# Every chunk of the wide layer is folded with six TensorE passes, and the scheduler's durations and offsets are fitted anew

## The chip, the cores and the metric

The program runs on one core of one Trainium2 chip. The metric is the device time of one execution in microseconds (us). Three runs of the kernel before took 1496.97, 1497.91 and 1501.18 us, a median of 1497.91.

## What is computed

The reference takes the real part of a two-dimensional FFT of eight batches of 3072 tokens by 256 columns, and feeds it to a wide layer and a soft mixture of eight experts:

```python
X = np.fft.fft(np.fft.fft(x, axis=1), axis=2).real        # 8 x 3072 x 256
h = X @ w_in;  g = h - np.tanh(h);  x = g @ w_out         # 256 -> 2048 -> 256
logits = x @ phi                                          # 32 slots
d = softmax of logits over the tokens;  slot_input = d.T @ x
slot_out[e] = relu(slot_input[e] @ w1[e]) @ w2[e]         # 8 experts of 4 slots
out = (softmax of logits over the slots) @ slot_out
```

## The kernel before, in words

The work has a head (weights are unpacked and combined), a main loop over 96 tiles (8 batches of 12), and a tail (experts, second softmax, output).

**A tile.** For every batch GpSimd (POOL) runs 24-point butterflies over the tokens in SBUF (`dft24`, recorded at L328, with scalings on ScalarE at L332). `z_dft` (L412 to L421) then makes one tile of 128 frequencies on TensorE. The input is real, so a tile stands for 128 tokens and their 128 mirrored tokens. Its two halves are the cosine part and the sine part of the columns; `z_high` and `z_low` split each into a high and a low float32r half.

**The wide layer.** It is done in four chunks of 512 columns per tile; a chunk's number is g, 384 in all, and its place in the tile is c = g % 4. With P the product of the cosine part and Q that of the sine part, the hidden values of a token and of its mirror are P + Q and P - Q. A product costs three passes of 512 columns on TensorE (high by high, high by low, low by high; `passes`, L463). There are two ways:

- *Folded*, three chunks in four: `wide` makes P (tile `pp`, doubled weights) and Q (`qq`) by three passes each. VectorE adds the term of column 128 to P (`evac`, L484) and makes the first sum (`plus`, L489); GpSimd subtracts to get the second (`minus`, L492). ScalarE takes tanh of both from SBUF (L501).
- *Whole*, the chunk with c = `FOLD` = 1: TensorE sums P + Q and P - Q itself, six passes for each, the second with sign-flipped weights `Wm`. ScalarE takes tanh in PSUM (L498). VectorE and GpSimd have nothing to do up to here.

Then, for every chunk and both signs, ScalarE writes the high float16 half of tanh (`act_t`, L509) and VectorE the low one (`low_t`, L513) into the ring `tr`. A DMA transpose on SyncE's queue (L517) turns the chunk into `tt`, and TensorE adds 16 small products to the logits (L544). After four chunks `slots` (L651) weighs the tile into the accumulator `ta`; every second tile the running softmax over tokens is carried on (L556 to L655). One of its instructions is `nm` (L589), a VectorE instruction on one column whose operands all lie in SBUF.

**What sets the order.** Every engine works through its own list in order. The lists are written when the program is built: the class `Flow` gets each operation with a duration, the rings of buffers that it takes and frees, and a place in a queue (`SCHED` holds one offset in chunks for each kind; `XLEAD`, `XSTEP`, `XEARLY`, `XFIRST` and `DSTEPS` place the loads and the butterflies of the next batch). It starts, again and again, the operation that can begin first by those durations. `HB` and `PB` are the numbers of buffers for the two sums (`h`) and for P (`pb`); `WB` is that of the PSUM banks that `pp` and `qq` may hold.

Of the kernel before, what the change touches and what calls it, by code (L numbers as in the profile page):

```python
# [46 lines left out]
SCHED = {
    "soft_t": 14.651, "logits": 6.337, "slots": 17.971, "soft_d": 16.201, "z_slots": 18.711, "z_turn": -1.458,
    "wide0": -0.165, "wide1": 0.725, "z_dft": -5.304, "ls_sum": 13.614, "soft_m": 15.558, "soft_h": 17.152,
    "soft_l": 17.462, "z_acc": 25.423, "evac": 1.54, "z_high": -2.259, "z_low": -1.816, "z_copy": -1.578,  # L50
    "z_turned": 1.314, "low_t0": 4.303, "low_t1": 5.258, "plus": 1.66, "minus": 2.729, "soft_e": 16.122,
    "ls_keep": 15.142, "act_h0": 2.255, "act_h1": 3.898, "act_t0": 3.417, "act_t1": 3.987, "acc_add": 28.127,
    "soft_x": 14.416,
# [173 lines left out]
def fft_mlp_softmoe_kernel(ctx: ExitStack, tc: tile.TileContext, x, w_in, w_out, phi, w1, w2, cq, fd, cm, ct, out):  # L227
# [439 lines left out]
    def s_wide():  # L667
        pp = pqs["S"] = bank("ppS", "pp")
        for n in range(4):
            for c in range(4):  # L670
                fs = slice(512 * c, 512 * c + 512)
                z, w = spec[0:1, 1, :], None
                if n < 2:
                    z, w = spec[:, 0, :], (Wh, Wl)[n][:, 0, fs].bitcast(F32)
                elif c == FOLD:
                    w = (Wh, Wl)[n - 2][0:1, 1, fs].bitcast(F32)
                elif n == 2:
                    w = W128[0:1, c - (c > FOLD), :]
                if w is not None:
                    nt.matmul(pp[32 * c:32 * c + 32, :], z, w, start=(n == 0), stop=(n == 2 + (c == FOLD)), tile_position=(0, 32 * c))  # L680

# [939 lines left out]
```

## Time and profile before

| | |
|---|---|
| median of three runs | 1497.91 us (1496.97 to 1501.18) |
| span of the profiled execution | 1494.0 us |
| head, until the first transposes of chunks | about 98 us |
| main loop | about 98 to 1353 us |
| tail | about 1353 to 1494 us |
| granted TensorE clock, mean | 0.983 (1.00 in the main loop) |

The span runs from the first to the last instruction of the profiled execution; the runs' times also hold what lies before and after it. A timeline row gives the start and the duration of an instruction. Durations of neighbours on one engine overlap: the next one starts before the one before has drained. What an instruction takes from its engine is the distance between starts, which is somewhat shorter than its duration.

### The profile page before, as it was taken

How to read it: one execution, taken by the hardware profiler on the slowest of the kernel's cores; microseconds unless marked ns; L12 is line 12 of the kernel's file. 1: busy time of each engine (PE TensorE's matmuls, PEld its weight loads, DVE VectorE, ACT ScalarE, POOL GpSimd, SP SyncE). 2: the span in 40 equal slices, each digit the busy share in tenths (PEclk: the TensorE clock that was granted, in tenths of full speed). 3: DMA queues.
4: the chain of work that ended last, by engine and by line, in shares of the span. 5: the costliest groups of instructions: out<-in, count | busy, mean ns of one | idle time of the engine just before them, and what ended most of it. 6: DMA issues, size and time to landing. Idle time of an engine off the chain costs nothing.

```text
span 1494.0 us, 38014 instructions
## 1 busy us (share of the span) xinstructions
PE 1410.3 (94%) x14636; PEld 1038.6 (70%) x14636; DVE 1170.2 (78%) x2041; ACT 1132.9 (76%) x2523; POOL 1012.2 (68%) x768
## 2 busy tenths in 40 slices
PE   4899999999999999999999999999999999996886
PEld 2577777777777777777777777777777776773464
DVE  7978878878878887888878788887878887783562
ACT  3467878878888778878887888878888877772476
POOL 5955799679968994899579956997599632231430
PEclk9999999999999999999999999999999999997898
DMA  7469999899999999999999999999999999899778
GB/s 229 138 155 198 195 202 196 149 193 179 195 178 197 177 187 185 187 180 188 178 184 191 186 187 176 201 169 190 171 193 181 199 188 186 156 199 294 243 296 366
DMA packets 856869, 292.90 MB, mean 196 GB/s; under 512 B 803440, under 2 KB 847344, under 8 KB 854896
## 3 DMA queue, kind: packets, MB, share of 16 engines
q1 hardware_dynamic: 856688, 290.47, 98.3%
q8 instruction: 115, 1.88, 0.5%
q14 instruction: 66, 0.54, 0.1%
HBM read 58.15 MB, written 30.67 MB: 59 GB/s over the span
## 4 chain that ended last, share of the span: by engine, by line
PE 85%; DVE 5%; DMA 5%; issue 2%; ACT 1%; SPq 0%; DVEq 0%
PE qq L463 22%; PE pp L463 22%; PE L L544 11%; PE ta L651 9%; DMA tt<-tr 3%; PE op L1546 3%; PE L L537 2%; PE tps L451 2%; PE zps L412 1%; PE zps L415 1%; PE zps L414 1%; PE zps L413 1%; PE LT L581 1%; PE zlp L635 1%; PE L L538 1%
## 5 line engine op out<-in xcount | busy, mean ns | idle before, releaser
L492 POOL TENSOR_TENSOR h<-pb,h 128x512 f32<-128x512 f32 x288 | 372.2, 1294 | 301.0 <-DVE h L489 289.2
L513 DVE SCALAR_TENSOR_TENSOR tr<-th,tr 128x512 f16<-128x512 f32 x576 | 382.3, 683 | 40.1 <-ACT tr L509 38.8
L463 PE MATMUL pp<-Wh,zh 128*128 128x512 f32 x960 | 374.3, 406 | 1.7 <-DVE tr L513 1.2
L501 ACT ACTIVATE th<-h 128x512 f32<-128x512 f32 x576 | 337.1, 607 | 38.9 <-DVE h L489 31.1
L509 ACT ACTIVATE tr<-th 128x512 f16<-128x512 f32 x576 | 335.3, 601 | 18.1 <-PE ta L651 8.4
L463 PE MATMUL qq<-Wh,zh 128*128 128x512 f32 x768 | 329.1, 428 | 3.6 <-DVE tr L513 3.5
L484 DVE SCALAR_TENSOR_TENSOR pb<-W,zts,pp 128x512 f32<-128x512 f32 x288 | 213.7, 742 | 54.2 <-PE pp L463 41.8
L489 DVE SCALAR_TENSOR_TENSOR h<-pb,qq 128x512 f32<-128x512 f32 x288 | 196.0, 681 | 64.5 <-PE qq L463 59.1
L544 PEld LDWEIGHTS <-tt 128*128 128x128 f16 x6144 | 194.0, 96 | 64.7 <-issue 49.2
L544 PE MATMUL L<-WPn,tt 128*128 128x64 f16 (+1 forms) x6144 | 225.8, 184 | 11.1 <-DMA tt<-tr 11.1
L463 PEld LDWEIGHTS pp<-Wh,zh 128*128 128x128 f32 x960 | 180.4, 188 | 46.1 <-DVE tr L513 5.3
L463 PE MATMUL pp<-Wl,zh 128*128 128x512 f32 x480 | 190.3, 396 | 0.0
L463 PEld LDWEIGHTS qq<-Wh,zh 128*128 128x128 f32 x768 | 145.0, 189 | 31.4 <-ACT zts L455 5.6
L328 POOL TENSOR_TENSOR xb<-xb 128x508 f32<-128x508 f32 (+3 forms) x103 | 146.2, 1422 | 30.0 <-DMA xb<-in_x 14.6
L463 PE MATMUL qq<-Wl,zh 128*128 128x512 f32 x384 | 151.4, 394 | 0.0
L651 PE MATMUL ta<-tr,dh 128*32 128x512 f16 x2304 | 145.3, 388 | 0.0
L442 ACT CAST zh<-zps 128x256 fp32r<-128x256 f32 x96 | 35.9, 374 | 100.3 <-PE zps L415 88.3
L651 PEld LDWEIGHTS <-dh 128*32 128x32 f16 x2304 | 54.4, 98 | 77.5 <-issue 32.8
L328 POOL TENSOR_TENSOR tA<-xb 128x1024 f32<-128x1024 f32 (+2 forms) x70 | 105.7, 1519 | 3.9 <-ACT xb L332 3.3
L463 PEld LDWEIGHTS pp<-Wl,zh 128*128 128x128 f32 x480 | 90.8, 189 | 14.8
L328 POOL TENSOR_TENSOR xb<-tA 128x508 f32<-128x508 f32 (+2 forms) x79 | 83.2, 1060 | 0.5
L463 PE MATMUL qq<-Wm,zh 128*128 128x512 f32 x288 | 83.3, 398 | 0.0
(266 smaller groups left out, 2448.3 us busy)
## 6 DMA issues: line engine op xcount, KB each, us to landing
out<-xb SPq DMA_DIRECT2D x14, 1536.0 KB, 6.2
xb<-in_x SPq DMA_DIRECT2D x32, 512.0 KB, 5.1
tr<-in_moe_w SPq DMA_DIRECT2D x16, 512.0 KB, 9.0
tt<-tr SPq DMA_TRANSPOSE x385, 4.9
xb<-in_moe_w SPq DMA_DIRECT2D x12, 512.0 KB, 4.4
raw<-in_moe_w_in SPq DMA_DIRECT2D x8, 512.0 KB, 3.6
xb<-in_x SPq DMA_DIRECT2D x16, 256.0 KB, 3.8
raw<-in_moe_w_out SPq DMA_DIRECT2D x8, 512.0 KB, 3.8
```

Of the source, the lines that this page charges most:

```text
L328: fn = lambda e: e.tensor_tensor(out=out[1](), in0=a[1](), in1=c[1](), op=op)
L442: ns.copy(out=z[1], in_=zpp[i])
L463: nt.matmul(o, z, v, start=first and n == 0, stop=last and n == 2)
L484: nv.scalar_tensor_tensor(out=pb, in0=W128[:, c - (c > FOLD), :], scalar=zs[i][3][:, 129:130], in1=pqs.pop((g, 0)), op0=ALU.mult, op1=ALU.add)
L489: nv.scalar_tensor_tensor(out=hs[g][:, 0, :], in0=pbs[g], scalar=0.5, in1=pqs.pop((g, 1)), op0=ALU.mult, op1=ALU.add)
L492: ng.tensor_tensor(out=hs[g][:, 1, :], in0=pbs.pop(g), in1=hs[g][:, 0, :], op=ALU.subtract)
L501: ns.activation(out=o, in_=hs[g][:, k, :], func=AF.Tanh)
L509: ns.activation(out=place_t(g)[:, 0, k], in_=ths[g, k], func=AF.Copy, scale=T14)
L513: nv.scalar_tensor_tensor(out=t[:, 1, k], in0=ths.pop((g, k)), scalar=T14, in1=t[:, 0, k], op0=ALU.mult, op1=ALU.subtract)
L544: nt.matmul(L[:, pm].rearrange("p b s -> p (b s)")[:, 0:n], tt[:, hl, pm, f, :], WPn[:, 4 * c + f].rearrange("p b s -> p (b s)")[:, 0:n], ...
L651: nt.matmul(tas[p][32 * c:32 * c + 32, :], dhl[p][:, dl, 2 * k + pm, :], ts[c][:, tl, pm, :], start=(k == 0 and n == 0), stop=(i == tiles( ...
L1546: nt.matmul(o.rearrange("p r d -> p (r d)"), c[:, j, :], R[:, 3 * h + k:3 * h + k + 2, :].rearrange("p r d -> p (r d)"), start=(h == 0), s ...
```

## The change

`whole`, the chunk of 12 passes, its weights `Wm` and its ways through `act_h`, `evac` and the scheduler go; `wide`, `evac`, `plus` and `minus` run for all 384 chunks. `W128` gets a fourth block. The freed SBUF holds a third buffer `pb` (`PB` 2 to 3). The durations that `Flow` reckons with, the offsets in `SCHED` and the places of loads and butterflies are other numbers, so all engines' lists are in another order. In the tail, two small tiles lie in other buffers.

```diff
-DSTEPS = 34.034
-XLEAD = -11.824
-XSTEP = 0.527
-XEARLY = 6.193
-XFIRST = 3.579
+DSTEPS = 17.994
+XLEAD = -7.457
+XSTEP = -11.057
+XEARLY = 36.171
+XFIRST = 11.84
 SCHED = {
...
-PB = 2
+PB = 3
...
-    def passes(o, zh, zl, w, first, last):
+    def passes(o, zh, zl, w):
         for n, (z, v) in enumerate(((zh, w[0]), (zh, w[1]), (zl, w[0]))):
-            nt.matmul(o, z, v, start=first and n == 0, stop=last and n == 2)
-
-    def whole(g):
-        return g % 4 == FOLD
+            nt.matmul(o, z, v, start=n == 0, stop=n == 2)
...
-        if n == 0 or whole(g):
-            passes(o, zh[:, 0, :], zl[:, 0, :], w[0], True, not whole(g))
-        if n == 1 or whole(g):
-            passes(o, zh[:, 1, :], zl[:, 1, :], (Wm[:, 0, :], Wm[:, 1, :]) if n and whole(g) else w[1], not whole(g), True)
+        passes(o, zh[:, n, :], zl[:, n, :], (Wh[:, n, fs], Wl[:, n, fs]))
...
     def act_h(g, k):
-        if whole(g):
-            o = ths[g, k] = pqs.pop((g, k))
-            ns.activation(out=o, in_=o, func=AF.Tanh, scale=0.5)
-        else:
-            o = ths[g, k] = bank(f"{PQN[k]}{g}", "th")
-            ns.activation(out=o, in_=hs[g][:, k, :], func=AF.Tanh)
+        o = ths[g, k] = bank(f"{PQN[k]}{g}", "th")
+        ns.activation(out=o, in_=hs[g][:, k, :], func=AF.Tanh)
...
-    def wide_x():
...
-    per_part(evac, {"V": 0.74}, lambda g: ([("pq", g, 0), ("zt", g // 4)], [("pb", g)], "pb", "w " + pb_(g)))
-    per_part(plus, {"V": 0.68}, lambda g: ([("pb", g), ("pq", g, 1)], [("h", g, 0)], "h", "v " + qb_(g)))
-    per_part(minus, {"G": 1.28}, lambda g: ([("pb", g), ("h", g, 0)], [("h", g, 1)], "", "pb"))
+    stage(evac, n4, 1, {"V": 0.67}, lambda g: ([("pq", g, 0), ("zt", g // 4)], [("pb", g)], "pb", "w " + pb_(g)))
+    stage(plus, n4, 1, {"V": 0.6}, lambda g: ([("pb", g), ("pq", g, 1)], [("h", g, 0)], "h", "v " + qb_(g)))
+    stage(minus, n4, 1, {"G": 1.28}, lambda g: ([("pb", g), ("h", g, 0)], [("h", g, 1)], "", "pb"))
...
-        stage(sub(low_t), n4, 1, {"V": 0.68}, lambda g: ([("th", g, k), ("t0", g, k)], [("t1", g, k)], "", b_(g)), f"low_t{k}")
+        stage(sub(low_t), n4, 1, {"V": 0.605}, lambda g: ([("th", g, k), ("t0", g, k)], [("t1", g, k)], "", b_(g)), f"low_t{k}")
```

TensorE, passes of the wide layer in the middle of the program, before: `pp` and `qq` of one whole chunk, six passes each (a number behind a name is the buffer).

```order
L463 MATMUL pp_7902<-Wh_84,zh_7799 128x512
L463 MATMUL pp_7902<-Wl_85,zh_7799 128x512
L463 MATMUL pp_7902<-Wh_84,zh_7799 128x512 x2
L463 MATMUL pp_7902<-Wl_85,zh_7799 128x512
L463 MATMUL pp_7902<-Wh_84,zh_7799 128x512
L463 MATMUL qq_7921<-Wh_84,zh_7799 128x512
L463 MATMUL qq_7921<-Wl_85,zh_7799 128x512
L463 MATMUL qq_7921<-Wh_84,zh_7799 128x512
L463 MATMUL qq_7921<-Wm_87,zh_7799 128x512 x3
```

TensorE in the changed kernel, at a like place (L461 is the same line; `dp` and `tps` are small products of the softmax and of a tile's turn):

```order
L461 MATMUL qq_8961<-Wh_84,zh_8770 128x512
L461 MATMUL qq_8961<-Wl_85,zh_8770 128x512
L461 MATMUL qq_8961<-Wh_84,zh_8770 128x512
L461 MATMUL pp_8975<-Wh_84,zh_8925 128x512
L461 MATMUL pp_8975<-Wl_85,zh_8925 128x512
L461 MATMUL pp_8975<-Wh_84,zh_8925 128x512
L449 MATMUL tps_8983<-cms_112,z32_8971 128x128 x2
L600 MATMUL dp_8987<-cms_112,dT_8928 128x128
L601 MATMUL dp_8987<-cms_112,dT_8928 128x128
```

Every `pp` and `qq` now has three passes; no product with `Wm` is left. The whole program has 2304 such passes where it had 2880.

GpSimd at the change from one batch's butterflies to the next one's, before (`xb_75` and `xb_76` are the two input buffers, `tA` and `tB` their scratch, `h<-pb,h` is `minus`):

```order
L328 TENSOR_TENSOR xb_75<-xb_75 128x512
L328 TENSOR_TENSOR tB<-xb_76 128x1024
L328 TENSOR_TENSOR tA<-xb_76 128x1024
L328 TENSOR_TENSOR xb_76<-xb_76,tA 128x1024
L492 TENSOR_TENSOR h<-pb,h 128x512 x9
L328 TENSOR_TENSOR tA<-xb_76,tA 128x1024
L328 TENSOR_TENSOR xb_76<-xb_76 128x4x127
L328 TENSOR_TENSOR xb_76<-tA 128x4x127
L492 TENSOR_TENSOR h<-pb,h 128x512 x2
```

GpSimd there in the changed kernel:

```order
L326 TENSOR_TENSOR xb_76<-xb_76 128x256
L326 TENSOR_TENSOR tA<-xb_75 128x1024
L483 TENSOR_TENSOR h<-pb,h 128x512 x2
L326 TENSOR_TENSOR xb_76<-xb_76 128x256 x2
L483 TENSOR_TENSOR h<-pb,h 128x512 x2
L326 TENSOR_TENSOR tB<-xb_75 128x1024
L326 TENSOR_TENSOR xb_75<-xb_75,tA 128x1024
L483 TENSOR_TENSOR h<-pb,h 128x512 x2
L326 TENSOR_TENSOR tA<-xb_75,tA 128x1024
L483 TENSOR_TENSOR h<-pb,h 128x512
L326 TENSOR_TENSOR xb_75<-xb_75 128x4x127
```

The stretch of nine `minus` (three tiles) without butterflies is gone: there are four between the first and the second butterfly of the new batch, and its first one stands ahead of the last ones of the batch before.

VectorE around `nm` (L589), before:

```order
L484 SCALAR_TENSOR_TENSOR pb_10198<-W128_86,zts_109,pp_10166 128x512
L655 SCALAR_TENSOR_TENSOR acc_68<-acc_68,fac_9816,ta_9956 128x512
L513 SCALAR_TENSOR_TENSOR tr_83<-th_10164,tr_83 128x512
L588 TENSOR_REDUCE mx_10246<-LT_10231 128x1
L589 SCALAR_TENSOR_TENSOR nm1_67<-mx_10246,ndesc_65,nm0_66 128x1
L513 SCALAR_TENSOR_TENSOR tr_83<-pp_10131,tr_83 128x512
L513 SCALAR_TENSOR_TENSOR tr_83<-th_10200,tr_83 128x512
```

VectorE there in the changed kernel (L475 is `evac`, L480 `plus`, L500 `low_t`, L576 `nm`):

```order
L480 SCALAR_TENSOR_TENSOR h_10220<-pb_10169,qq_10171 128x512
L500 SCALAR_TENSOR_TENSOR tr_83<-th_10175,tr_83 128x512
L475 SCALAR_TENSOR_TENSOR pb_10250<-W128_86,zts_108,pp_10216 128x512
L500 SCALAR_TENSOR_TENSOR tr_83<-th_10177,tr_83 128x512
L575 TENSOR_REDUCE mx_10269<-LT_10252 128x1
L576 SCALAR_TENSOR_TENSOR nm1_67<-mx_10269,ndesc_65,nm0_66 128x1
L500 SCALAR_TENSOR_TENSOR tr_83<-th_10247,tr_83 128x512
```

`low_t` no longer reads `pp` directly (no whole chunk), and an `evac` and a `plus` stand on VectorE for every chunk; `nm` has the same neighbours as before.

## Rows read from the trace of the kernel before

**Rows 1.** Page, part 1: busy us, share of the span, instructions.
```profile
PE 1410.3 (94%) x14636; PEld 1038.6 (70%) x14636; DVE 1170.2 (78%) x2041; ACT 1132.9 (76%) x2523; POOL 1012.2 (68%) x768
```
**Rows 2.** Busy by window: us, PE, PEld, DVE, ACT, POOL (x count), clock, DMA share, GB/s.
```profile
353.30:391.25 37.95, 37.95 (x425) 28.21 (x424) 30.89 (x52) 30.86 (x72) 37.19 (x33) 1.00 0.96 178
568.35:593.65 25.30, 25.30 (x284) 19.32 (x284) 20.81 (x38) 20.97 (x45) 7.76 (x6) 1.00 1.00 166
618.37:775.73 157.36, 155.89 (x1716) 116.15 (x1720) 128.67 (x223) 128.50 (x291) 124.83 (x95) 1.00 1.05 184
1196.20:1345.50 149.30, 149.30 (x1670) 110.12 (x1671) 117.85 (x214) 113.32 (x243) 42.65 (x33) 1.00 1.00 182
```
**Rows 3.** The same window, L328 (butterflies) alone: us, DVE, POOL, then as above.
```profile
618.37:775.73 157.36, 0.00 (x0) 79.95 (x59) 1.00 1.05 184
```
**Rows 4.** The chain that ended last, in order of time: start, us, what.
```profile
614.34 1.41 PE pp L463 x6
615.74 0.44 PE L L544 x16
616.18 1.49 PE qq L463 x6
617.67 0.69 PE pp L463 x3
618.37 1.41 PE ta L651 x24
...
775.73 1.41 PE ta L651 x24
```
**Rows 5.** Timeline of VectorE: start, duration, engine, line, operation.
```profile
610.37 0.68 DVE L489 SCALAR_TENSOR_TENSOR h<-pb,qq 128x512 f32<-128x512 f32 x1
610.96 0.74 DVE L484 SCALAR_TENSOR_TENSOR pb<-W,zts,pp 128x512 f32<-128x512 f32 x1
611.62 0.69 DVE L513 SCALAR_TENSOR_TENSOR tr<-qq,tr 128x512 f16<-128x512 f32 x1
612.22 0.68 DVE L489 SCALAR_TENSOR_TENSOR h<-pb,qq 128x512 f32<-128x512 f32 x1
```
**Rows 6.** Timeline of GpSimd, around 655 and 979 us.
```profile
655.29 1.30 POOL L492 TENSOR_TENSOR h<-pb,h 128x512 f32<-128x512 f32 x1
656.53 1.45 POOL L328 TENSOR_TENSOR tA<-xb 128x256 f32<-128x256 f32 x2
...
979.36 1.29 POOL L492 TENSOR_TENSOR h<-pb,h 128x512 f32<-128x512 f32 x1 [2.22 <-DVE h L489]
```
**Rows 7.** Groups by line: count | busy us, mean ns | idle before it, releaser.
```profile
L492 POOL TENSOR_TENSOR h<-pb,h 128x512 f32<-128x512 f32 x288 | 372.2, 1294 | 301.0 <-DVE h L489 289.2 <-ACT tr L509 4.5 <-ACT d L621 3.0
L501 ACT ACTIVATE th<-h 128x512 f32<-128x512 f32 x576 | 337.1, 607 | 38.9 <-DVE h L489 31.1 <-POOL h L492 3.5 <-DVE pb L484 0.2
L498 ACT ACTIVATE qq<-qq 128x512 f32<-128x512 f32 x96 | 56.3, 587 | 7.2 <-PE qq L463 7.2
L589 DVE SCALAR_TENSOR_TENSOR nm<-mx,ndesc,nm 128x1 f32<-128x1 f32 x49 | 40.5, 826 | 1.7
```
**Rows 8.** Timelines of VectorE (`nm`) and GpSimd, around 608 and 974 us.
```profile
608.70 0.22 DVE L589 SCALAR_TENSOR_TENSOR nm<-mx,ndesc,nm 128x1 f32<-128x1 f32 x1
...
974.08 3.07 DVE L589 SCALAR_TENSOR_TENSOR nm<-mx,ndesc,nm 128x1 f32<-128x1 f32 x1
...
973.54 2.37 POOL L328 TENSOR_TENSOR xb<-xb 128x1024 f32<-128x1024 f32 x1
975.88 1.25 POOL L328 TENSOR_TENSOR xb<-xb,tA 128x512 f32<-128x512 f32 x1
```
**Rows 9.** The tile `tt`, DMA transposes on SyncE's queue: duration ns min/median/max.
```profile
L517 SPq DMA_TRANSPOSE tt<-tr x384: 1315/2370/4782, 97.9 to 1356.5; - x192
```

More of the change, by code (lines that the diff above doesn't have):

```diff
@@ L38 @@
 NQ = 12
-FOLD = 1
-DSTEPS = 34.034
-XLEAD = -11.824
-XSTEP = 0.527
-XEARLY = 6.193
-XFIRST = 3.579
-SCHED = {
[L48 to L53, printed above, removed]
+DSTEPS = 17.994
[3 more added lines that the diff above has]
+XFIRST = 11.84
+SCHED = {
+    "soft_t": 14.736, "logits": 6.122, "slots": 17.943, "soft_d": 16.071, "z_slots": 18.144, "z_turn": -0.947,
+    "wide0": -0.101, "wide1": 0.864, "z_dft": -9.332, "ls_sum": 13.23, "soft_m": 15.89, "soft_h": 17.424,
+    "soft_l": 17.504, "z_acc": 23.039, "evac": 1.126, "z_high": -8.198, "z_low": -6.035, "z_copy": -1.871,
+    "z_turned": 0.619, "low_t0": 3.814, "low_t1": 5.183, "plus": 2.397, "minus": 2.799, "soft_e": 15.977,
+    "ls_keep": 13.707, "act_h0": 2.714, "act_h1": 3.836, "act_t0": 3.351, "act_t1": 4.523, "acc_add": 23.725,
+    "soft_x": 14.22,
 }
@@ L668, in s_wide @@
         pp = pqs["S"] = bank("ppS", "pp")
-        for n in range(4):
+        for n in range(3):
             for c in range(4):
-                fs = slice(512 * c, 512 * c + 512)
-                z, w = spec[0:1, 1, :], None
                 if n < 2:
[L674 to L680, printed above, removed]
+                    z, w = spec[:, 0, :], (Wh, Wl)[n][:, 0, 512 * c:512 * c + 512].bitcast(F32)
+                else:
+                    z, w = spec[0:1, 1, :], W128[0:1, c, :]
+                nt.matmul(pp[32 * c:32 * c + 32, :], z, w, start=(n == 0), stop=(n == 2), tile_position=(0, 32 * c))
     def s_tanh():
@@ L850, in wide_w @@
         for kk in range(2):
-            l = (fds[:, kk, 0:128], fds[:, kk, 128:256] if c == FOLD else fdz[:, kk, :], Y["f128"][:, 0, :])[k]
+            l = (fds[:, kk, 0:128], fdz[:, kk, :], Y["f128"][:, 0, :])[k]
             nt.matmul(o, l, win[c][:, kk, :], start=(kk == 0), stop=(kk == 1))
     def wide_c(c, k):
-        sc = 1.0 if k == 1 and c != FOLD else 2.0
-        o, out = (Y["W", c, k], Wh[:, k, 512 * c:512 * c + 512]) if k < 2 else (Y.pop(("W", c, k)), W128[:, c - (c > FOLD), :])
+        sc = 2.0 - (k == 1)
+        o, out = (Y["W", c, k], Wh[:, k, 512 * c:512 * c + 512]) if k < 2 else (Y.pop(("W", c, k)), W128[:, c, :])
         ns.activation(out=out, in_=o, func=AF.Copy, scale=sc)
@@ L861, in wide_l @@
         fs = slice(512 * c, 512 * c + 512)
-        sc = 1.0 if k == 1 and c != FOLD else 2.0
+        sc = 2.0 - (k == 1)
         nv.scalar_tensor_tensor(out=Wl[:, k, fs], in0=Y.pop(("W", c, k)), scalar=sc, in1=Wh[:, k, fs].bitcast(F32),
                                 op0=ALU.mult, op1=ALU.subtract)
-    def wide_x():
-        fs = slice(512 * FOLD, 512 * FOLD + 512)
-        for k, w in enumerate((Wh, Wl)):
-            ns.activation(out=Wm[:, k, :], in_=w[:, 1, fs].bitcast(F32), func=AF.Copy, scale=sgn)
     def win_t(c, h):
@@ L968, in w_units @@
                     both = [("wi", c, 0), ("wi", c, 1)]
-                    for j in range(3 if c != FOLD else 2):
+                    for j in range(3):
                         hf.add({"T": 1.8}, lambda _, c=c, j=j: wide_w(c, j), ["fdz"] + both, [("W", c, j)], take=B("W", c, j))
@@ L1097, in w128_unit @@
         if k == 0:
-            late_consts.append(wbp.tile([128, 1536], F32, tag="W128", name="w128w"))
+            late_consts.append(wbp.tile([128, 2048], F32, tag="W128", name="w128w"))
             ny.dma_start(out=late_consts[0][:, 0:608], in_=ct)
@@ L1168, in fft_mlp_softmoe_kernel @@
-    parts = [g for g in range(n4) if not whole(g)]
-    def per_part(fn, cost, keys):
-        for g in parts:
-            r, w, take, free = keys(g)
-            put(g, cost, lambda e, g=g: fn(g), r, w, take, free, 0.0, fn.__name__)
-    pb_, qb_ = (lambda g, n=n: f"B:{n}{g}" for n in PQN)
-    stage(lambda g: wide(g, 0), n4, 1, kind({"T": 0.77}, {"T": 1.54}), lambda g: ([("zh", g // 4)], [("pq", g, 0)], f"+B w {pb_(g)}", ""), "wide0")
-    stage(lambda g: wide(g, 1), n4, 1, kind({"T": 0.77}, {"T": 1.54}), lambda g: ([("zh", g // 4)], [("pq", g, 1)], f"+B v {qb_(g)}", ""), "wide1")
```

32 lines of the change are left out of this document (14 added, 18 removed).

## The prediction

> **What bounds the kernel now.** I read the page's busy times first [rows 1]. TensorE (PE) is busy for 94% of the span, VectorE (DVE) for 78%, ScalarE (ACT) for 76%, GpSimd (POOL) for 68%. These are means over head, loop and tail, so the loop has to be read by itself. The chain of waits gives the loop's clock: `ta` comes once a tile, and from its start at 618.37 us to that at 775.73 us lie twelve tiles, one batch [rows 4]. A batch thus takes 157.36 us and a tile 13.1 us. In that window TensorE is busy 155.89 us, 99% of it, VectorE 128.67, ScalarE 128.50 and GpSimd 124.83 [rows 2]. So the loop is bound by TensorE, and the others have about 29 to 33 us to spare in each batch. GpSimd's spare time is uneven: where it has no butterflies it works 7.76 of 25.30 us, elsewhere 37.19 of 37.95 us, and TensorE shows no gap in either [rows 2]. In the window of the last batch GpSimd ran 33 instructions, all of them `minus`, three for each of 11 tiles; there TensorE fills the whole 149.30 us [rows 2].
>
> **The change, part by part, for one batch of twelve tiles.**
>
> *TensorE loses passes.* A whole chunk has twelve, a folded one six, and one chunk in four was whole: six passes fewer per tile. Six passes in a row take 1.41 us [rows 4], 0.235 us each. Twelve tiles save 72 x 0.235 = 16.9 us: 155.89 - 16.9 = 139.0 us. For the program it is 576 passes and 135 us. If TensorE stayed the bound, that would be the gain.
>
> *VectorE gets `evac` and `plus` for the fourth chunk.* By distance between starts, `evac` takes 0.66 us (610.96 to 611.62) and `plus` 0.59 (610.37 to 610.96) or 0.60, as `low_t` beside it does [rows 5]: 1.26 us per tile, 15.1 per batch. 128.67 + 15.1 = 143.8 us. This is a high figure, because the busy time of a row includes the draining of instructions after which the engine idles, and that goes when it is denser.
>
> *GpSimd gets `minus` for it.* 655.29 to 656.53 is 1.24 us [rows 6]; twelve make 14.9. 124.83 + 14.9 = 139.7 us, of which the butterflies are 79.95 [rows 3]. Before, this work could not be spread evenly: three tiles at each change of batch held none. In the changed order the next batch's butterflies begin there, so 139.7 is a mean that nearly every stretch has, about 11.6 us per tile.
>
> *ScalarE* takes the same number of tanh, two per tile from SBUF (607 ns) in place of PSUM (587 ns) [rows 7]: 24 x 0.02 = 0.5 us, 129.0 per batch. It is no bound.
>
> *SyncE's queue* keeps its transposes. A batch has 48 of a median 2.37 us [rows 9], 114 us, besides loads and stores. They fit into 140 us and more, but with less room; the price of a late one is in the third case below.
>
> *At nothing:* in the head the second chunk gets a third weight product and one more ScalarE copy and loses two sign flips on ScalarE; a ScalarE instruction of 512 columns is 0.6 us [rows 7], so I take the balance as 2 us either way. It is hidden beside the unpacking of the weights on VectorE; without that cover it would be those 2 us. The two tiles that move in the tail add no transfer. The third `pb` lets VectorE run further ahead of GpSimd and costs no instruction.
>
> *The sum.* The engine that ends last is VectorE at 143.8, with GpSimd at 139.7 and TensorE at 139.0 just behind it. So the bound moves off TensorE, and only part of its 16.9 us can be had: at most 157.4 - 139.7 = 17.7 us, if VectorE's figure shrinks, at least nothing, if the three hold each other up by more than 13.6 us. No row shows three engines this full at once. The nearest row has two: GpSimd at 98% while TensorE is at 100% (353.30 to 391.25) [rows 2]. I take that 98% for VectorE: 143.8 / 0.98 = 146.7 us per batch, 10.7 us less than now. Seven batches have butterflies beside them: 7 x 10.7 = 75 us. The last has none: TensorE 149.30 - 11 x 1.41 = 133.8, VectorE 117.85 + 11 x 1.26 = 131.7 [rows 2]; with the same 98%, 136.5, a gain of 13 us. The profiled span of 1494.0 us becomes 1494 - 75 - 13 = 1406; the median of the runs lies 3.9 us above that span, so I expect 1410 us.
>
> **The rivals.**
>
> *B: nothing is lost between the engines.* VectorE's figure shrinks under GpSimd's 139.7, and a batch takes that. Gain 7 x 17.7 + 15.5 = 139 us: 1359 us. For it: TensorE reaches 99% of a window today. Against it: it does so while every other engine has a fifth of its time to spare, and it never had to wait for them.
>
> *C: GpSimd has to wait for `plus`.* Today it idled 301 us ahead of its 288 `minus`, nearly all for VectorE's `h` [rows 7]: 1.05 us each, free while it has 33 us per batch to spare. With 139.7 us of work and a fixed order such a wait is no longer free: at 979.36 it stood 2.22 us for `plus` with butterflies still to do [rows 6]. If 0.25 us for each of the 48 `minus` of a batch remain, the batch takes 139.7 + 12 = 151.7: 7 x 5.7 = 40 us, and about 10 in the last batch: 1448 us. A transpose that comes late would act alike.
>
> *D, slower: VectorE's `nm` is shut out by GpSimd.* `nm` works on one column. While GpSimd idles it takes 0.22 us (608.70); at 974.08 it took 3.07 us, past the end of a butterfly that had begun before it (973.54 + 2.37) and through the next one (975.88 + 1.25) [rows 8]. Its mean is 0.826 us [rows 7]. The changed GpSimd list has hardly a gap left, and `nm` stands on the engine that would now be last, with `low_t` queued behind it, for which the transposes and the logits wait; ScalarE's exponentials wait for `nm` itself. A batch has six. VectorE has 157.36 - 143.8 = 13.6 us until nothing is gained, so D decides from 0.826 + 13.6 / 6 = 3.1 us per `nm`, about the worst row of today, on average. Passed over by one instruction more (1.24 us) it would be 4.3: 143.8 + 6 x 3.5 = 164.8 us, 7.4 more than now in seven batches, less 13 in the last: 1498 + 52 - 13 = 1537 us.
>
> On this the Trainium skill has a rule (SBUF — State Buffer, section "Who interferes with whom"): a VectorE instruction with two SBUF inputs contends with a GpSimd instruction that reads SBUF, and whichever issues first holds the shared ports for its whole instruction. By that rule `nm` waits for the rest of one instruction at most. The row at 974.08 agrees that it waits, but shows that it can lose to the following instruction as well; by the rule alone the sum stays as it is, by the row taken for every `nm` the gain is gone. `evac`, `plus` and `low_t` have one input in PSUM, and their distances of 0.59 to 0.66 us while GpSimd worked [rows 5] show no such wait.
>
> That the change would not do what it says can be left aside: the changed TensorE list has 2304 passes for 2880.
>
> **How the numbers follow.** The forecast (about 1380 to 1440 us) gets 0.55, B 0.13, C 0.20. D gets 0.08: six stalls at today's worst are needed in every batch to reach even the turning point, where the mean today is a quarter of that. Between C and D, where waits eat just what is saved, lies no change, 0.04. A measurement of this kernel can tell about 0.3% from no change, which is 4.5 us around 1497.9. So faster 0.88, same 0.04, slower 0.08. For eight in ten the range reaches from near B's 1359 through C: 1362 to 1480 us; outside lie D, no change and the far ends of B and C. The forecast's own range stands above.
>
> **What would show it right or wrong.** Right: in a batch's window TensorE is busy about 139 us and VectorE over 140, with VectorE's share the highest at 95% or more; GpSimd has no stretch at a third of its time but in the last batch; `ta` comes every 12.2 us. TensorE's idle time appears ahead of `pp` and `qq` and names VectorE, since the banks come free late. Wrong: GpSimd idles 10 us or more per batch ahead of `minus` (C), or `nm` has a mean over 2 us (D), or TensorE is still busy for 98% (B, or less saved than the passes say). A longer head or tail would be a part that I costed at nothing.

## The result: faster, by half of what was forecast

| | median us | runs | profiled span us |
|---|---|---|---|
| kernel before | 1497.44 | 1496.9 to 1501.18 | 1494.0 |
| changed kernel | 1451.84 | 1448.11 to 1453.38 | 1449.2 |
| forecast | 1410 (1362 to 1480) | | 1406 |

The ratio is 0.9694, with a 95% interval from 0.9671 to 0.9716. The kernel gained 46 us where 88 were forecast. The time lies inside the range, and it lies almost on the price of rival C (1448).

The first view of the changed kernel is part 1 of its page: busy us, share of the span, instructions. It answers to [rows 1].

```profile
PE 1308.9 (90%) x14062; PEld 950.3 (66%) x14062; DVE 1275.5 (88%) x2233; ACT 1137.5 (78%) x2522; POOL 1127.6 (78%) x864
```

TensorE lost 101 us of busy time, VectorE gained 105, GpSimd 115, ScalarE 5. The second view is the windows of batches, as in [rows 2]: start and end, length, then PE, PEld, DVE, ACT and POOL busy, the granted clock of TensorE, the DMA share, GB/s. They run from the first `low_t` of a batch to that of the next: the shortest of the seven that have butterflies, one in the middle, the longest, and the last batch.

```profile
398.70:544.30 145.60, 140.99 (x1633) 103.55 (x1626) 141.96 (x248) 129.67 (x291) 138.45 (x106) 1.00 1.10 194
544.30:693.60 149.30, 141.11 (x1638) 104.29 (x1637) 140.62 (x249) 127.97 (x291) 138.18 (x106) 0.99 1.12 193
842.20:997.50 155.30, 145.47 (x1634) 108.05 (x1626) 145.09 (x249) 129.43 (x291) 139.18 (x107) 0.96 1.07 187
1152.00:1295.40 143.40, 137.61 (x1602) 99.82 (x1602) 129.39 (x236) 115.68 (x255) 68.65 (x58) 0.98 1.07 193
```

The work per batch is what the prediction summed: TensorE 141 us, VectorE 141 to 142, GpSimd 138. What is not as forecast is the length, 150.9 us on average over seven batches where 146.7 were expected. No engine is busy for 98% of any of them. The next two views name what is waited for. The waits of the whole run are given as engine and line, what it waited for, us in total, times, longest us. From the view of the tile `tt` come the duration of its transposes (ns, min/median/max, on SyncE's queue), the waits for it, and the us from issue to landing.

```profile
POOL h L483 <- DVE h L480: 151.1, 129, 6.2
ACT th L488 <- DVE h L480: 64.2, 104, 2.4
PEld L531 <- DMA tt<-tr: 62.7, 73, 3.6
PEld L531 <- issue: 45.7, 157, 0.5
PE L L531 <- DMA tt<-tr: 39.8, 41, 3.3
```

```profile
L504 SPq DMA_TRANSPOSE tt<-tr x384: 1316/2485/5124, 99.5 to 1308.8; - x192
...
  DMA tt<-tr: 102.5, 114
...
DMA to landing us min/median/max: 3.3/5.0/8.1
```

The view of the tile has 102.5 us of waits for transposes that had not landed. It adds the waits of TensorE's weight loads (PEld, 62.7 us) and of its matmuls (PE, 39.8 us), and by their times these are the same waits, seen twice. So what the matmuls lost to late transposes is 39.8 us, in 41 waits. Before, the sum is 25.6 us, and the matmuls' own part:

```profile
PE L L544 <- DMA tt<-tr: 11.1, 10, 3.3
```

A transpose took a median of 2.37 us there [rows 9]; now it is 2.485. The page's chain of work that ended last says the same as shares of the span, by engine and then by line:

```profile
PE 49%; DVE 19%; DMA 19%; issue 6%; ACT 5%; POOL 1%; SPq 0%; DVEq 0%; ACTq 0%; POOLq 0%
DMA tt<-tr 17%; PE pp L461 10%; PE qq L461 10%; PE L L531 6%; PE ta L638 6%; DVE tr L500 5%; DVE pb L475 3%; DVE h L480 3%; PE op L1511 3%; ACT th L488 2%; ACT tr L496 1%; PE L L524 1%; PE zps L410 1%; PE tps L449 1%; PE zlp L622 1%
```

The chain of before by engine:

```profile
PE 85%; DVE 5%; DMA 5%; issue 2%; ACT 1%; SPq 0%; DVEq 0%
```

Before, TensorE held 85% of this chain and the transposes 3%. Now nothing holds half of it. The groups by line (count, busy us, mean ns, idle time ahead and its releaser) answer to [rows 7]:

```profile
L483 POOL TENSOR_TENSOR h<-pb,h 128x512 f32<-128x512 f32 x384 | 493.0, 1289 | 166.6 <-DVE h L480 151.1 <-ACT tr L496 6.0 <-ACT z L430 4.6
L475 DVE SCALAR_TENSOR_TENSOR pb<-W,zts,pp 128x512 f32<-128x512 f32 x384 | 283.2, 739 | 24.1 <-PE pp L461 14.3 <-ACT zts L453 8.3
L480 DVE SCALAR_TENSOR_TENSOR h<-pb,qq 128x512 f32<-128x512 f32 x384 | 259.7, 678 | 14.3 <-PE qq L461 7.7 <-ACT tr L496 2.5 <-ACT th L488 1.9
L576 DVE SCALAR_TENSOR_TENSOR nm<-mx,ndesc,nm 128x1 f32<-128x1 f32 x49 | 48.0, 979 | 1.7
```

The last view shows SyncE's queue: start, us, and operations of a kind that follow on one another, with their count.

```profile
591.60 14.03 SPq L504 DMA_TRANSPOSE tt<-tr  x5
605.72 0.63 SPq L550 DMA_DIRECT2D lsd<-lsw  x1
606.46 22.51 SPq L504 DMA_TRANSPOSE tt<-tr  x8
629.02 0.84 SPq L550 DMA_DIRECT2D lsd<-lsw  x1
630.34 10.56 SPq L504 DMA_TRANSPOSE tt<-tr  x4
```

Seventeen transposes and two stores stand here in 49.3 us (591.60 to 640.89); by the single records there is one pause of 1.1 us among them and no other of 0.5: 2.9 us of the queue per chunk, where TensorE, VectorE and GpSimd need 2.9 to 3.0 (141/48, 142/48 and 138/48). **SyncE's queue is a fourth resource that is as full as the engines**, and no line of busy times shows it. I added up all DMA records of that queue between 250 and 1150 us, with the gaps of under 0.3 us between one and the next. This "held" share is used below. It says that the queue is taken, not what keeps it so long; that question comes behind e12.

| kernel | issues us | short gaps us | held, of 900 us | matmuls' waits for `tt`, whole run, us | median us |
|---|---|---|---|---|---|
| before | 744.2 | 30.0 | 86% | 11.1 | 1497.4 |
| changed | 802.8 | 35.6 | 93% | 39.8 | 1451.8 |
| e1 | 834.5 | 40.3 | 97% | 54.9 | 1429.7 |
| e2 | 434.2 | 19.1 | 50% | 0.9 | 1417.8 |
| e8 | 453.6 | 19.2 | 53% | 1.0 | 1357.8 |
| e9 | 834.2 | 60.9 | 99% | 74.5 | 1494.1 |
| e11 | 840.5 | 40.9 | 98% | 53.1 | 1424.0 |
| e12 | 793.3 | 31.8 | 92% | 48.8 | 1418.9 |

### The profile page after: what moved, and what is told of

Same layout as the page of the kernel before. It is cut to its first block, busy times and chain, and to the rows that moved or that the text cites. A ratio compares the mean times of both kernels' runs of the same rounds, so it can differ in the third digit from the quotient of the medians.

```text
span 1449.2 us, 37232 instructions
## 1 busy us (share of the span) xinstructions
PE 1308.9 (90%) x14062; PEld 950.3 (66%) x14062; DVE 1275.5 (88%) x2233; ACT 1137.5 (78%) x2522; POOL 1127.6 (78%) x864
## 4 chain that ended last, share of the span: by engine, by line
PE 49%; DVE 19%; DMA 19%; issue 6%; ACT 5%; POOL 1%; SPq 0%; DVEq 0%; ACTq 0%; POOLq 0%
DMA tt<-tr 17%; PE pp L461 10%; PE qq L461 10%; PE L L531 6%; PE ta L638 6%; DVE tr L500 5%; DVE pb L475 3%; DVE h L480 3%; PE op L1511 3%; ACT th L488 2%; ACT tr L496 1%; PE L L524 1%; PE zps L410 1%; PE tps L449 1%; PE zlp L622 1%
## 5 line engine op out<-in xcount | busy, mean ns | idle before, releaser
L483 POOL TENSOR_TENSOR h<-pb,h 128x512 f32<-128x512 f32 x384 | 493.0, 1289 | 166.6 <-DVE h L480 151.1
L488 ACT ACTIVATE th<-h 128x512 f32<-128x512 f32 x768 | 455.2, 610 | 86.7 <-DVE h L480 64.2
L500 DVE SCALAR_TENSOR_TENSOR tr<-th,tr 128x512 f16<-128x512 f32 x768 | 508.2, 680 | 7.6 <-ACT tr L496 6.3
L496 ACT ACTIVATE tr<-th 128x512 f16<-128x512 f32 x768 | 440.9, 602 | 11.7 <-PE ta L638 4.9
L461 PE MATMUL qq<-Wh,zh 128*128 128x512 f32 x768 | 334.4, 435 | 12.1 <-DVE tr L500 8.1
L461 PE MATMUL pp<-Wh,zh 128*128 128x512 f32 x768 | 323.3, 421 | 14.8 <-DVE tr L500 3.7
L475 DVE SCALAR_TENSOR_TENSOR pb<-W,zts,pp 128x512 f32<-128x512 f32 x384 | 283.2, 739 | 24.1 <-PE pp L461 14.3
L480 DVE SCALAR_TENSOR_TENSOR h<-pb,qq 128x512 f32<-128x512 f32 x384 | 259.7, 678 | 14.3 <-PE qq L461 7.7
L531 PEld LDWEIGHTS <-tt 128*128 128x128 f16 x6144 | 197.1, 96 | 110.4 <-DMA tt<-tr 62.7
L531 PE MATMUL L<-WPn,tt 128*128 128x64 f16 (+1 forms) x6144 | 231.2, 185 | 41.0 <-DMA tt<-tr 39.8
L461 PEld LDWEIGHTS pp<-Wh,zh 128*128 128x128 f32 x768 | 147.1, 192 | 58.3 <-DVE tr L500 7.2
L461 PEld LDWEIGHTS qq<-Wh,zh 128*128 128x128 f32 x768 | 147.6, 192 | 43.8 <-DVE tr L500 11.5
L461 PE MATMUL pp<-Wl,zh 128*128 128x512 f32 x384 | 153.9, 401 | 0.0
L461 PE MATMUL qq<-Wl,zh 128*128 128x512 f32 x384 | 153.7, 400 | 0.0
L461 PEld LDWEIGHTS pp<-Wl,zh 128*128 128x128 f32 x384 | 74.0, 193 | 9.0
L461 PEld LDWEIGHTS qq<-Wl,zh 128*128 128x128 f32 x384 | 74.4, 194 | 3.0
L326 POOL TENSOR_TENSOR tB<-xb 128x256 f32<-128x256 f32 (+1 forms) x47 | 72.4, 1547 | 3.2 <-ACT xb L330 3.1
```

The lines of the kernel that those rows point to most:

```text
L326: fn = lambda e: e.tensor_tensor(out=out[1](), in0=a[1](), in1=c[1](), op=op)
L461: nt.matmul(o, z, v, start=n == 0, stop=n == 2)
L475: nv.scalar_tensor_tensor(out=pb, in0=W128[:, c, :], scalar=zs[i][3][:, 129:130], in1=pqs.pop((g, 0)), op0=ALU.mult, op1=ALU.add)
L480: nv.scalar_tensor_tensor(out=hs[g][:, 0, :], in0=pbs[g], scalar=0.5, in1=pqs.pop((g, 1)), op0=ALU.mult, op1=ALU.add)
L483: ng.tensor_tensor(out=hs[g][:, 1, :], in0=pbs.pop(g), in1=hs[g][:, 0, :], op=ALU.subtract)
L496: ns.activation(out=place_t(g)[:, 0, k], in_=ths[g, k], func=AF.Copy, scale=T14)
```

## The experiments

Ratios are to the kernel before, run on the same chip. Its medians there ran from 1493.3 to 1498.8 us, so a difference in us between two versions is good to some 5 us. By the ratios, the gains on the changed kernel are 20 us (e1), 32, 15, 12 and 17 (e2 to e5), 95 (e8), 29 (e11) and 30 us (e12). Where an expected text speaks of the waits for `tt` (102 or 145 us, under 40, 60 or 80), it means the sum of the view, with weight loads and matmuls. All but e6, e7 and e11 keep the changed kernel's order on TensorE, VectorE, ScalarE and GpSimd (in e9 and e10 but for the eight products of `logits`, in e12 but for the DMAs that ScalarE issues). The first four tell apart theory V (VectorE is the bound), D (the transposes end last) and P (GpSimd).

**e1: `nm` with one SBUF input.**

```diff
-        LT = lts[p] = halves(bank(f"LT{p}", "LT", 256))
+        o = bank(f"LT{p}", "LT")
+        LT, mxs[p] = halves(o[:, 0:256]), o[:, 256:257]
...
-        mx = sp.tile([128, 1], F32, tag="mx", name="mx")
+        mx = mxs.pop(p)
```

> The changed kernel, but the running maximum's new value `mx` is kept in a spare PSUM column of its bank, so that `nm` has one SBUF input in place of two. In the changed kernel `nm` takes 979 ns on average, 49 times; without GpSimd it took 219 ns, so at most 37 us leave VectorE. Theory V (VectorE is the bound and holds the others up): `nm` falls to about 0.25 us and 20 to 37 us are gained, 1415 to 1432 us. Theory D (the DMA transposes of `tt` come last, TensorE waits for them): 0 to 8 us. Theory P (GpSimd's `minus` and butterflies are the bound): 0 to 8 us.

Measured: 1429.73 us, ratio 0.9557 [0.9532, 0.9581], 22 us under the changed kernel. The row of `nm` (ns, min/median/max), in the changed kernel and then in e1:

```profile
L576 DVE SCALAR_TENSOR_TENSOR nm<-mx,ndesc,nm x49: 218/808/3879, 134.0 to 1316.6; 128x1 f32<-128x1 f32 x49
```

```profile
L578 DVE SCALAR_TENSOR_TENSOR nm<-LT,ndesc,nm x49: 217/219/222, 132.9 to 1297.2; 128x1 f32<-128x1 f32 x49
```

With `mx` in PSUM all 49 take 0.22 us under the same GpSimd load. The wait was for GpSimd, and here it takes two inputs in SBUF to bring it on. It holds VectorE for 37 us in all (48.0 less 49 x 0.22). The gain lies in the range of theory V and not in those of D and P. But the matmuls' waits for `tt` grew to 54.9 us (145.3 in the sum of the view): the next bound stands right behind.

**e2: half a transpose.** Only the high half of `t` is transposed, and `logits` uses it twice; the low half's share is left out.

```diff
-            out=tt.rearrange("p a b c d -> p (a b c) d"), in_=tq[g].rearrange("p a b f -> p (a b f)")
+            out=tt[:, 0].rearrange("p b c d -> p (b c) d"), in_=tq[g][:, 0].rearrange("p b f -> p (b f)")
...
-                        ... tt[:, hl, pm, f, :],
+                        ... tt[:, 0, pm, f, :],
```

> The changed kernel, but only the high float16 half of each chunk is transposed, and the logits use it in place of the low half too (the low half's share is left out); TensorE, VectorE, ScalarE and GpSimd do the same work in the same order, each transpose moves half the bytes. Theory D: the 102 us that TensorE's queue waited for `tt` mostly go, 30 us or more are gained, under 1422 us. Theory V: under 10 us, 1442 to 1452 us. Theory P: the same, under 10 us.

Measured: 1417.80 us, 0.9482 [0.9461, 0.9503], 34 us under the changed kernel. The tile `tt`, and the window of 900 us in the loop (columns as above):

```profile
L504 SPq DMA_TRANSPOSE tt<-tr x384: 1231/1237/2512, 98.7 to 1279.1; - x192
...
  DMA tt<-tr: 2.0, 3
...
DMA to landing us min/median/max: 3.0/3.2/5.7
```

```profile
250.00:1150.00 900.00, 863.78 (x9987) 638.12 (x9985) 871.02 (x1507) 783.55 (x1762) 841.55 (x643) 0.99 0.61 112
```

The waits for `tt` are gone, and only now is VectorE at 97%, the 98% that I had taken for it. This is the range of D and not that of V, as e1's was that of V and not that of D: neither is the one bound. The gain of 34 us is near the 39.8 us that the matmuls had stood. The transposes end last, and VectorE stands right behind them. The edit takes away time on the queue, bytes and 1.8 us of landing at once; e9 and e12 ask which of them counts.

**e3: `minus` on 256 of 512 columns** (ScalarE's tanh reads these twice; the other half of the result is left out).

```diff
-        ng.tensor_tensor(out=hs[g][:, 1, :], in0=pbs.pop(g), in1=hs[g][:, 0, :], op=ALU.subtract)
+        ng.tensor_tensor(out=hs[g][:, 1, 0:256], in0=pbs.pop(g)[:, 0:256], in1=hs[g][:, 0, 0:256], op=ALU.subtract)
```

> The changed kernel, but `minus` computes 256 of the 512 columns and ScalarE's tanh of the second sum reads them twice (half of the second sums are left out); 384 times about 0.6 us leave GpSimd, 230 us in all, 2.4 us per tile; nothing else changes. Theory P: 40 us or more are gained, under 1412 us. Theory V: up to 12 us, since `minus` comes earlier for ScalarE, 1440 to 1452 us. Theory D: under 8 us.

**e4: `plus` on 256 of 512 columns**, with the readers of `h` reading these twice, as in e3; half of the sums is left out.

```diff
-nv.scalar_tensor_tensor(out=hs[g][:, 0, :], in0=pbs[g], scalar=0.5, in1=pqs.pop((g, 1)), ...
+nv.scalar_tensor_tensor(out=hs[g][:, 0, 0:256], in0=pbs[g][:, 0:256], scalar=0.5, in1=pqs.pop((g, 1))[:, 0:256], ...
```

> The changed kernel, but `plus` computes 256 of the 512 columns, which ScalarE's tanh and GpSimd's `minus` read twice (half of the first sums are left out); 384 times about 0.27 us leave VectorE, 103 us in all, 1.07 us per tile. Theory V: 40 to 75 us are gained, until TensorE with 139 us per batch is the bound, 1377 to 1412 us. Theory D: under 10 us. Theory P: under 10 us, and more idle time on VectorE.

**e5: fewer passes.** One chunk in four leaves out the product of the low part of z, 4 passes for 6.

```diff
...
-        passes(o, zh[:, n, :], zl[:, n, :], (Wh[:, n, fs], Wl[:, n, fs]))
+        passes(o, zh[:, n, :], zl[:, n, :], (Wh[:, n, fs], Wl[:, n, fs]), 2 if c == 1 else 3)
```

> The changed kernel, but in one chunk of four (c = 1) both products are made with two passes, without the low half of z (that share is left out); 192 passes of 0.235 us, 45 us in all, 0.47 us per tile, leave TensorE. If TensorE is still a bound, 30 to 45 us are gained, 1407 to 1422 us. If it is not, as the forecast had it, under 12 us: 1440 to 1452 us.

Measured: e3 1433.74 us, 0.9597 [0.9571, 0.9624]; e4 1438.0, 0.9613 [0.9581, 0.9646]; e5 1437.32, 0.9582 [0.9532, 0.9633]. The window of the loop in e3 and in e4:

```profile
250.00:1150.00 900.00, 849.64 (x9831) 624.28 (x9827) 853.34 (x1483) 770.72 (x1735) 674.02 (x632) 0.99 1.10 194
```

```profile
250.00:1150.00 900.00, 852.81 (x9856) 631.76 (x9851) 801.35 (x1485) 771.69 (x1743) 830.81 (x633) 0.99 1.09 194
```

e3 takes GpSimd to 75%, e4 VectorE to 89%, e5 takes 2 of 6 passes off every fourth chunk of TensorE, and each gains only 18, 14 and 15 us on the changed kernel's median. The matmuls' waits for `tt` stay at 44.8, 43.1 and 55.7 us. All three miss every range that was expected: each gain is far below the 30 us and more of a single bound, and above the 8 to 12 us of an engine that is none, in e4 and e5 by less than the noise. Lightening any one engine is worth little; V and P fall as the single bound, and e3's 18 us are more than D by itself allows.

**e6 and e7: the fold and the fit apart.** e6 has the new fold with before's durations, offsets and number of `pb`; e7 has before's whole chunk with the new durations and offsets, and two `pb`.

```diff
-XLEAD = -7.457
+XLEAD = -11.824
-    "soft_t": 14.736, "logits": 6.122, "slots": 17.943, ...
+    "soft_t": 14.651, "logits": 6.337, "slots": 17.971, ...
...
-PB = 3
+PB = 2
```

> One part alone: every chunk folded, with the numbers of before (all durations, offsets, places of loads and butterflies, and two buffers pb). If the gain of 46 us comes from the passes and the fit only refines it: 1445 to 1475 us. If the fit is what makes the fold pay (GpSimd, which has 13 us more per batch, and VectorE with 15, keep the old uneven order): 1480 us or more, up to slower than before.

> The other part alone: one chunk in four with 12 passes as before, with the new durations, offsets and places, two buffers pb. TensorE keeps its 156 us of work per batch and was busy 99% of it, so no gain by the forecast's reasons: 1488 to 1505 us. A gain of over 10 us would mean that the fit is worth something by itself; over 1510 us that the new order fits the new work only.

Measured: e6 1578.86 us, 1.0530 [1.0484, 1.0575], slower than before; e7 1513.84, 1.0087 [1.0061, 1.0114]. The longest waits of e6:

```profile
POOL h L483 <- DVE h L480: 245.2, 157, 13.6
PEld L531 <- DMA tt<-tr: 130.0, 129, 3.4
PE L L531 <- DMA tt<-tr: 94.5, 92, 3.2
ACT zh L440 <- PE zps L413: 74.2, 63, 4.6
DVE zh L444 <- ACT zh L440: 60.8, 34, 10.4
```

Here SyncE's queue was held for only 80%, and yet VectorE stops up to 10.4 us for `zh`, and the matmuls wait 94.5 us in all for `tt`. With a queue that has room I put this down to the order. Less work in an order that was made for other durations costs 5%; the fold is worth its gain only with the fit, and the fit alone is worth nothing. Which part of the fit carries it, the durations, the offsets or the third `pb`, was not tried.

**e8: e1 and e2 together**, the low half's share of `logits` left out as in e2.

> The two edits that gained most together: `mx` in PSUM (gained 22 us by itself) and transposes of the high half only (33 us by itself; the logits' low share is left out). If the two waits are separate (a stall on VectorE, a late transpose on SyncE's queue), the gains add: 1390 to 1402 us. If both only uncover the same next bound, VectorE's 97%, 1408 us or more.

Measured: 1357.76 us, 0.9061 [0.9024, 0.9097], 94 us under the changed kernel where the single gains, 22 and 34, sum to 56.

```profile
250.00:1150.00 900.00, 893.32 (x10509) 660.87 (x10507) 873.30 (x1579) 818.60 (x1847) 854.36 (x655) 1.00 0.64 118
```

TensorE is back at 99%, with VectorE at 97%. The seven batches take 140.7 us on average. Both ranges that were expected (1390 to 1402, and 1408 or more) are missed: together the two edits bring more than their sum. It is rival B's price (1359): without these two waits hardly anything is lost between the engines. Each alone brings little, because the other was the next to end last.

**e9: the transpose in two halves**, of which the high half can go out as soon as ScalarE has written it and the queue is free. **e10** is e9 with e1's `mx`.

```diff
-        ny.dma_start_transpose(out=tt..., in_=tq[g]...)
+        for k in range(2):
+            ny.dma_start_transpose(out=tt[:, k]..., in_=tq[g][:, k]...)
...
-        for f in range(4):
-            for pm in range(2):
-                for hl in range(2):
+        for hl in range(2):
+            for f in range(4):
+                for pm in range(2):
```

> The transpose of each chunk goes out as two, the high half (which ScalarE has written earlier) ahead of the low one, and logits takes its eight high products first; all is computed. The order on PE, VectorE, ScalarE and GpSimd stays as it is but for these eight. Theory T (the logits wait because the one transpose can be issued only when VectorE has written the low half, then holds the queue for 2.485 us and lands 5.0 us after the issue): the low half alone is left behind that point, with 1.24 us of the queue, and the high products cover 0.8 us more, so it is ready some 2 us earlier against waits of 1.1 us mean; the waits on tt fall from 102 us to under 40, and the time comes near the run with half a transpose: 1417 to 1430. Rival Q (what counts is the queue's load of 2.485 us in every 3.1 us, so that a late one pushes on the next): two halves cost the queue as much or more, and the waits stay at 90 to 120 us: 1445 to 1465.

> The split transposes of the run before together with mx in PSUM; all is computed. If the two waits together are what the changed kernel loses (the run with both removed gave 1357.8) and the split takes the transposes' part: 1360 to 1385, far below the sum of the single gains (22 and at most 33 us, which would give 1397). If the queue's load counts (Q): no better than mx alone, 1425 to 1440.

Measured: e9 1494.11 us, 0.9976 [0.9953, 1.0]; e10 1491.9, 0.9973 [0.9954, 0.9993]. All of the gain is gone. e9's transposes:

```profile
L505 SPq DMA_TRANSPOSE tt<-tr x768: 1231/1287/4250, 98.6 to 1353.5; - x192
...
  DMA tt<-tr: 171.0, 246
...
DMA to landing us min/median/max: 3.1/3.5/6.8
```

A half lands sooner (3.5 us for 5.0), and yet TensorE waits longer (74.5 us for the matmuls). In the 900 us the halves held the queue for a mean of 1.426 us, two of them 2.85 where the whole one held it for 2.60, and the queue is at 99%. T fell and Q held, beyond its range: the load of the queue sets the pace, not how early a single transpose can start. With the queue full, e10's shorter `nm` is worth nothing; its 1491.9 us lie above both ranges that were expected.

**e11: e1, and the planner told that a transpose lands 3 us after its issue.**

```diff
-        put(g + 0.001, {"D": 2.4}, ..., [("tt", g)], "tt", "", 2.0, "low_t1")
+        put(g + 0.001, {"D": 2.4}, ..., [("tt", g)], "tt", "", 3.0, "low_t1")
```

> mx in PSUM, and the planner's landing time of a transpose raised from 2.0 to 3.0 us, with which it plans the order anew on every engine; all is computed. If the logits were only planned too early, they move back by 1 us against waits of 1.1 us mean, and tt waits fall below 60 us: 1375 to 1405. If the numbers fit together only as a set (the new fold with the old numbers gave 1578.9), a replanned order gives back what the waits gain: 1420 to 1470.

Measured: 1424.01 us, 0.9503 [0.9473, 0.9534]. It lies at the fast end of the second theory's range (1420 to 1470). It is 6 us under e1, with intervals that just overlap, and the waits for `tt` went only from 145 to 134 us in the sum, from 54.9 to 53.1 for the matmuls. A later place for `logits` doesn't make room in a queue that is held for 98%.

**e12: e1, and the loads of x and the stores of `lsw` issued by ScalarE.**

```diff
-                ny.dma_start(out=xb[:, 8 * a + c:8 * a + c + n, :], ...
+                (ns if b else ny).dma_start(out=xb[:, 8 * a + c:8 * a + c + n, :], ...
...
-        ny.dma_start(out=lsd_of(b)[:, 2 * n:2 * n + 4, :], in_=lsw[p])
+        ns.dma_start(out=lsd_of(b)[:, 2 * n:2 * n + 4, :], in_=lsw[p])
```

> mx in PSUM as in the run e1_nm_psum, and the loads of x after the first and the stores of lsw are issued by ScalarE instead of SyncE, so that SyncE issues transposes alone; all is computed, the order is otherwise that of e1_nm_psum (1429.7). In that run SyncE's queue is held for 834.5 us of issues and 40 us of gaps between them in the 900 us from 250 to 1150, 97% (changed kernel: 93%, kernel before: 86%), 56 us of it by loads and stores. Theory S (the holding of SyncE's queue is the bound): some 60 us of 900 come free, and the waits for tt fall from 145 to under 80 us: 1375 to 1405. Rival E (what holds the queue is the 256-byte packets of the transposes behind it, 2048 each, and not the issue): the transposes are held as much longer as the queue was freed, by about 0.15 us each, and the time stays at 1420 to 1440. Rival A (ScalarE, 779 us of 900 busy, stops in order at the 78 issues): slower than 1440.

Measured: 1418.9 us, 0.9496 [0.9449, 0.9543]. It has the lowest median of the versions that compute everything, 33 us under the changed kernel, though its interval overlaps that of e11.

```profile
L504 SPq DMA_TRANSPOSE tt<-tr x384: 1316/2606/5493, 96.6 to 1276.5; - x192
...
  DMA tt<-tr: 118.7, 119
...
DMA to landing us min/median/max: 4.3/5.2/9.2
```

ScalarE did not lose by it (787.55 us busy of 900), so rival A fell. Neither S nor E came out: the queue went from 97% to 92%, the waits from 145 to 119 us in the sum, and 11 us came of it where S wanted 25 to 55 (9 us by the ratios, whose intervals just overlap). The transposes took 0.03 us more on average (2.689 for 2.662 us), not the 0.15 of E.

**What keeps the queue so long stays open.** A rival stands: that the 16 DMA engines behind the queue are full, and the queue only waits for them. The windows of the loop of the changed kernel, e9 and e12 (the last two figures are the DMA share and GB/s):

```profile
250.00:1150.00 900.00, 848.95 (x9737) 625.11 (x9739) 848.52 (x1470) 768.31 (x1724) 821.80 (x623) 0.98 1.09 192
250.00:1150.00 900.00, 831.78 (x9455) 609.57 (x9456) 827.25 (x1425) 746.16 (x1669) 798.77 (x606) 0.98 1.08 186
250.00:1150.00 900.00, 859.70 (x10028) 634.82 (x10016) 841.06 (x1514) 787.55 (x1775) 843.36 (x644) 1.00 1.12 198
```

e9 speaks for the queue: the DMA engines move no more than in the changed kernel, the queue goes from 93% to 99%, and the time is lost. e12 speaks against the queue by itself: 5% of it came free, and the matmuls still wait 48.8 us, with the DMA share at 1.12 as in e1. That the transposes end last is shown by e2; whether a whole one is held up on the queue or behind it is not.

## Why the prediction was half right

**TensorE, VectorE, GpSimd and ScalarE: right.** Per batch 139.0, 143.8, 139.7 and 129.0 us were forecast; in the windows above with butterflies stand 141 to 145, 141 to 145, 138 to 139 and 128 to 130. TensorE's passes cost what was said: at the full clock of 398.70:544.30 it had 141.0 us. Its busy time over the whole run fell by 101 us only, where the sum has 135. In e8 the same number of TensorE instructions had 1273.1 us, 137 less than before, at a mean granted clock of 0.988 for 0.969. So the passes were priced rightly, and the other 36 us are time that the changed kernel adds to the same work.

**The signs.** TensorE's idle time was to stand ahead of `pp` and `qq` and to name VectorE. Of the two groups' 26.9 us VectorE's `low_t` ended 11.8; ahead of `L` the matmuls stood 39.8 us for `tt`. VectorE was to have the highest share, 95% or more; in the loop it has 94%, as TensorE does.

**SyncE's queue: the step that failed.** It said: "A batch has 48 of a median 2.37 us [rows 9], 114 us, besides loads and stores. They fit into 140 us and more, but with less room". Three things were mis-sized. The median isn't the mean: in the loop of before a transpose held the queue for 2.512 us on average, 48 of them 120.6. The "besides" was not priced: 53.4 us of loads and stores in 900 us (744.2 - 690.8 of transposes), 9.3 per batch. And the short gaps are 5.2. That makes 135 us, not 114, and in a forecast batch of 146.7 it would have been 92% of the queue, nearly as full as the engines for which I did weigh the loss. It then grew to 140 us per batch (93% of 150.9), with a transpose at 2.598 us. A transpose that follows within 0.3 us on the queue takes longer (2.60 us on average in before, 171 of them) than one behind a pause of over 2 us (1.93 us, 14 of them), and in the changed kernel 229 follow so closely. By the sum over the records, with its mean and all that shares the queue, the fourth full resource was there to be seen before.

**The 2% for holding each other up: too small by a factor of three.** VectorE's 141 to 142 us lie in batches of 150.9, so 6% was lost. e8 shows of what: with transposes half as long and `nm` free of GpSimd the batch is 140.7 us. The row at 98% from which I took the loss had two full engines, and a queue that was held for 80% of that stretch. In the sum this makes 146.7 into 150.9: seven batches gained 46 us (from an average of 157.5) for 75 forecast, the last one 6 for 13. Head and tail, costed at nothing, took some 7 us more (1494.0 - 1449.2 = 44.8, of 52 in the batches): 2 us of it lie ahead of the first `low_t`, 5 behind the last. What these 5 are was not tried.

**Rival C: its price came out by luck; its main cause did not.** GpSimd does wait for `plus`, 151 us in all, 129 times, which was my sign for C. But e3, which takes 148 of GpSimd's 822 us in the window away, gains 18 us: its waiting is not what costs the most. The sentence "A transpose that comes late would act alike" named the cause that carries the weight (e2: 34 us), and it deserved a case with a sum of its own. The measured time lies inside my range only because the range is wide: the work was forecast rightly, and the loss between the engines was not.

**Rival D: the mechanism is right, its price is not in the mean.** `nm` came to a mean of 0.979 us, far from the turning point of 3.1, so D did not decide. By the mean the excess over 0.22 us is 37 us in the run; e1 gave 22 alone, and behind e2 60 (1417.8 to 1357.8). In e2 `nm` had a mean of 1.173 us, an excess of 47 us. What the other 13 are was not separated; TensorE's busy time fell by 26 us too (1299.4 to 1273.1), at a mean granted clock of 0.988 for 0.971. On the rule of the Trainium skill (SBUF — State Buffer, "Who interferes with whom"): that two SBUF inputs are what makes it contend is borne out by e1, 49 of 49 at 0.22 us. What I drew from its lock, that the wait is one GpSimd instruction at most, is not borne out: [rows 8] and the 3.879 us here, more than the longest GpSimd instruction of the loop (2.44 us), decide against it.

**B was right about the engines.** In e8, where no transpose and no `nm` stops them, hardly anything is lost between them: TensorE is busy for 99%.

## What to carry to other kernels

Where a change moves work off the one full engine, add up every in-order queue, the DMA queues too, with means and not medians, and with everything that shares the queue: in the table a queue held for 86% went with 11 us of waits, one held for 92% and more with 40 us and more. Weigh a queue that will be that full as you would an engine. When several resources are nearly full at once, taking the load off one is worth little, and two waits taken away together can be worth more than their sum; try them in pairs. And an order written by a planner belongs to its durations: less work in the old order was 5% slower than before.
